# The end of the first block: additions to x ahead of the row scale's copy, and the row scale's fetch ahead of raw weight loads

## The chip, the cores and the metric

The kernel runs on one core of a Trainium2 chip. The metric is the device time of one execution in microseconds (us). Three runs of the kernel before took 599.77, 598.26 and 590.91 us; the median is 598.26. The core's engines are TensorE (PE: matmuls into PSUM banks), VectorE (DVE), ScalarE (ACT), GpSimd (POOL) and SyncE (SP). The last three also issue DMA transfers, each in the order of its own program.

## The reference

Two layers share one layernorm of x (2048 rows of 1024) and their results are added to x. The first is a diagonal complex state space model, the second a dense layer with the Mish activation.

```python
xn = layernorm(x)
# A: Lam_bar = exp(dt * Lam);  B_bar = ((Lam_bar - 1) / Lam)[:, None] * B
Bu = einsum("bld,pd->blp", xn, B_bar)
h[t] = Lam_bar * h[t - 1] + Bu[t]
a = 2 * einsum("blp,dp->bld", h, C).real + xn * Dskip
# B: w1 is 1024 x 3584, w2 is 3584 x 1024
m = mish(xn @ w1 + b1)
return x + a + m @ w2
```

## The kernel before, in words

**Blocks.** The 2048 rows are worked in four blocks of 512 (L1801 and on). Block 0 uses plain matmuls. In block 1 the product with B, and a part of the product with w1, are done in 2 x 2 halves with seven products instead of eight; the products are named by a letter and a number (`a2` is form 2 of the pair a). In blocks 2 and 3 all of w1 is done so. The seven products need sums and differences of halves of the weights, in f16, so the weights are first scaled by powers of two.

**Units of w1.** w1 is cut into seven units of 512 columns, numbered 0 to 6. A unit goes through a chain: `w_load` (L1089, four raw loads at L1096 on GpSimd's queue), `w_scale` (L1160, two scalings at L1163 on ScalarE, then three stores of raw parts to `wsd` in DRAM at L1157 on GpSimd), and `w_sums` (L1170, four sums at L1178 on VectorE, each followed by a store at L1157). The first sum writes over the raw part whose store is the third of `w_scale`. SyncE then loads the forms from `wsd` into the seven slots of `ring` (L457), in the order in which TensorE uses them. Unit 3 is loaded first at the end of block 0, then unit 4; units 5 and 6 follow in block 1, their loads standing on GpSimd's queue behind the stores of unit 3's sums.

**The row scale.** B's rows are scaled by powers of two before the seven products of block 1. `rows_scale` (L1726) works the scales out on VectorE and writes them to DRAM as `scd` (L1745); `rows_fetch` (L1748, the DMA at L1749) fetches them, spread over all partitions; `rows_spread` (L1753, the copy at L1754) puts them in order on VectorE; `scale_B` (L1766, products at L1771) multiplies B by them. Each is done for two halves. For half 0 the write and the fetch stand on GpSimd's queue, for half 1 on ScalarE's.

**The end of block 0.** `tail` (L1461) adds up the block's eight PSUM banks; its last matmuls (L1468) read the scanned state. `finish` (L1654) then adds two banks to a quarter of x on VectorE (L1665) and stores the result from ScalarE's queue (L1651). TensorE's next work is `first_tile` (L866): twelve tiles of w1 for block 1, of eight matmuls each (L873), tile f in bank f modulo 8; ScalarE empties each with Mish (L881). After them come the products of B in the order of `WHOLE` (L190: a2 a1 b2 b1 a5 b5 ...) at L950 and those of the units at L1022. The pair a uses banks 4 to 6 and the pair b banks 0 to 2: b2 writes bank 1, b1 bank 0, b5 bank 2.

**What sets the order.** Each engine's instructions are recorded in the order in which the Python program calls them, and run in that order; an instruction waits for the events of the buffers it reads and writes (`Queue`, L91 and on). `side(f)` (L1805) interleaves other work with the tiles: with tile 0 the sums of units 3 and 4 and the loads of units 5 and 6, and with tile 7 `w_scale(5)`, which on ScalarE thus stands ahead of emptying tiles 8 to 11.

Of the kernel before, what the change touches and what calls it, by code (L numbers as in the profile page):

```python
# [163 lines left out]
def build_kernel(nc, A_x, A_Lambda_re, A_Lambda_im, A_B_re, A_B_im, A_C_re, A_C_im,  # L164
# [16 lines left out]
    FAST = 1  # L181
# [95 lines left out]
    def c(n):  # L277
        return cs[:, CN.index(n), :]
# [963 lines left out]
    def some(n):  # L1242
        for _ in range(n):
            (steps or later).pop(0)()
# [481 lines left out]
    def rows_scale(h):  # L1726
        hs = slice(NJ // 2 * h, NJ // 2 * (h + 1))
        ab0, ab1, ss, si = (c(n)[:, hs] for n in ("ab0", "ab1", "ss", "si"))
        e8, f8 = si_i[:, 0, hs], si_i[:, 1, hs]
        b_a, b_e, b_f = b_ab[0][h], b_si_i[0][h], b_si_i[1][h]  # L1730

        def power(o, b_o, src, b_s, m, a):
            vop(lambda e: e.tensor_scalar(f8, src, m, a, op0=ALU.mult, op1=ALU.add), reads=[b_s], writes=[b_f])
            vop(lambda e: e.tensor_scalar(o.bitcast(i32), f8, 23, None, op0=ALU.logical_shift_left), reads=[b_f], writes=[b_o])

        vop(lambda e: e.tensor_tensor(ab0, ab0, ab1, op=ALU.add), reads=[b_a, b_ab[1][h]], writes=[b_a])
        vop(lambda e: e.tensor_scalar(ab0, ab0, 2.0 ** 100, 2.0 ** -100, op0=ALU.min, op1=ALU.max),
            reads=[b_a], writes=[b_a])
        vop(lambda e: e.tensor_scalar(e8, ab0.bitcast(i32), 24, None, op0=ALU.logical_shift_right),
            reads=[b_a], writes=[b_e])  # L1740
        power(ss, b_ss[h], e8, b_e, -2.0, 2.0 * 127 + 9)
        vop(lambda e: e.tensor_copy(sbf[:, hs], ss), reads=[b_ss[h]], writes=[b_sbf[h]])
        power(si, b_si[h], e8, b_e, 1.0, 59.0)
        power(ab1, b_ab[1][h], e8, b_e, -1.0, 195.0)
        (AC if h else PO).dma(lambda e: e.dma_start(scd[h], sbf[:, hs]), DmaSem(nc, "d_scd%d" % h),  # L1745
                              reads=[b_sbf[h]], writes=[b_scd[h]])
# [56 lines left out]
    for blk in range(NB):  # L1803

        def side(f):  # L1805
            if blk:
                if f == 0:
                    snaps_ready()
                    scale_B(1, (1,))
                    w_sums(3)  # L1810
                    w_load(5)
                    sums_B(0)
                    for n in range(4):
                        sums_x(blk, n)
                    sums_B(1)
                    w_load(6)
                    rows_spread(1)
                    scale_B(2)
                    w_sums(4)
                    scale_B(3)  # L1820
                if f in (1, 3, 4, 5):
                    table_scale((1, 3, 4, 5).index(f))
                if f == 7:
                    w_scale(5)
                    w_sums(5, True)
                ring_fill()
                return
            if f == 2:
                turn_sines()
            if f == NR:  # L1830
                aop(lambda e: e.activation(act[:, 0:NR, 0:2 * P], hraw[:, 0:NR, :], AF.Mish),
                    reads=b_hbf[0:4], writes=b_actf[0:NR])
            if f in (19, 27):
                for j in range(4):
                    table(j + (4 if f > 19 else 0))
            if f in (5, 6, 7, 8):
                coefficients(f - 5)
            if f in (8, 9, 11, 12):
                ln_skip(0, (8, 9, 11, 12).index(f))
            if f in turns:  # L1840
                transpose_B(turns.index(f))
            if f >= 26:
                transpose_C(f - 26)
            if f == 9:
                for h in range(2):
                    w_most(2, h)
            if f >= 12 and f % 4 < 2:
                w_most(f // 4, f % 4)
            if f in (23, 25, 26, 27):
                ln_stats_only(1, (23, 25, 26, 27).index(f))  # L1850
            if f == 26:
                w_row(0)
                w_spread(0)

        for x, f in enumerate(() if blk in SPLIT else TILES if blk == FAST else range(NF)):
            first_tile(blk, f)
            side(x)

        near = 0 < blk < NB - 1
        out_stage = tail(blk, n_item[0] + (len(W_ITEMS) if blk in SPLIT else len(OPENS) // 2 if blk == FAST else 0))  # L1860
        open_unit = next(out_stage)
        if blk in SPLIT:
            project_fast(blk, STEPS if near else LAST, open_unit)
        elif blk:
            project_fast(blk, WHOLE, open_unit)
        else:
            project_in()
        if blk == FAST:
            for q in range(NQ):
                next_stats(blk + 1, q)  # L1870
        if blk in SPLIT:
            next(out_stage)
            if near:
                next(out_stage)
        for j in range(NJ):
            if blk == 0 and j == NJ - 1:
                rows_scale(0)
                w_load(3)
                rows_fetch(0)
            if blk == 0 and j == 0:  # L1880
                w_exponent(0)
            recur(blk, j)
            if blk == FAST and j == 0:
                next_root()
                for q in range(NQ):
                    next_scale(blk + 1, q)
            if blk in SPLIT:
                if near and j == 0:
                    act_sums(blk, ((4, 0),))
                    next(out_stage)  # L1890
                if near and j in (2, 4, 7):
                    some(4)
                if j == 6:
                    vop(lambda e: e.tensor_tensor(KS[:, 1, :, :], KS[:, 1, :, :], KS[:, 3, :, :], op=ALU.add),
                        reads=[b_KS[1], b_KS[3]], writes=[b_KS[1]])
                continue
            if blk:
                if j == 0:
                    next(out_stage)
                    w_load(2)  # L1900
                    for i in range(2):
                        w_abs(i)
                    w_row(1)
                    w_spread(1)
                    w_scale(2)
                if j == 5:
                    w_exponent(1)
                    row_bound()
                    for i in range(2):
                        w_scale(i)  # L1910
                continue
            if j == 0:
                ln_root()
                for q in range(NQ):
                    ln_scale(1, q)
            scale_C(j)
            if j:
                keep_C(j - 1)
            if j < 3:
                next(out_stage)  # L1920
            if j < 4:
                for g in ((7,), (8,), (9, 10), (11,))[j]:
                    row_sizes(g)
            if j == 3:
                next(out_stage)
                for i in range(NHS):
                    rows_load(i)
                rows_size(0)
                rows_size(1)
                row_sizes(12)  # L1930
                rows_size(2)
                row_sizes(13)
                next(out_stage)
            for i in {4: (3, 4), 5: (5, 6, 7), 6: (8, 9, 10, 11), 7: range(12, 16)}.get(j, ()):
                rows_size(i)
        if near:
            for q in range(NQ):
                ln_skip(blk + 1, q)
            for n in range(4):
                sums_x(blk + 1, n)  # L1940
        if 0 < blk < NB - 1:
            carry()
        if blk == SPLIT[0]:
            uncarry()
        if blk == FAST:
            w_sums(2, True)
            some(4)
            for i in (0, 1):
                w_sums(i, True)
        if blk == FAST - 1:  # L1950
            keep_C(NJ - 1)
            w_load(4)
            rows_scale(1)
            for n in ("c1", "s1"):
                PO.op(lambda e, n=n: e.tensor_tensor(c(n), c(n), c("ab1"), op=ALU.mult), reads=[b_cs[n]] + b_ab[1], writes=[b_cs[n]])
            carry(PO)
            rows_spread(0)
            scale_B(0)
            scale_B(1, (0,))
            w_scale(3)  # L1960
            rows_fetch(1)
            w_scale(4)
        for _ in out_stage:
            pass

    SP.wait(out_events.values())

# [33 lines left out]
```

## Time and profile before

| what | value |
| --- | --- |
| median of three runs | 598.26 us |
| profiled execution, its own time | 598.32 us |
| its span | 597.1 us |
| TensorE busy | 583.7 us, 98% of the span |
| VectorE busy | 503.1 us, 84% |
| ScalarE busy | 403.5 us, 68% |
| GpSimd busy | 153.7 us, 26% |
| mean granted clock of TensorE | 0.997 |

The span runs from the first to the last instruction; the execution's own time is 1.2 us longer. A row of a timeline gives the start in us, the length in us, the engine, the line of the kernel, the operation, what is written and what is read, how many instructions are merged in the row, and in brackets how long the engine had stood idle and what ended that. In the chain of waits a row has the start, the length and what the chain ran through. In a list of waits a row has who waited for whom, the total in us, how often, and the longest. The granted clock is the share of TensorE's full rate that the chip allowed it.

### The profile page before, as it was taken

The page shows a single profiled execution, that of the slowest core. Times are in us where ns is not written, and L with a number is a line of the kernel's source. Part 1 is how long each engine was busy: PE and PEld are TensorE (multiplying, and loading weights), DVE is VectorE, ACT ScalarE, POOL GpSimd, SP SyncE. Part 2 cuts the span into 40 slices and gives each one's busy share as a digit, 9 for nine tenths or more (in the row PEclk, how much of TensorE's full clock was granted, in tenths as well). Part 3 has the DMA queues.
Part 4 walks back from the last instruction along what each step waited for, and adds up shares of the span by engine and source line. Part 5 has one row for each costly group of instructions (what it writes and reads, how often), then busy time and mean ns, then how long its engine had stood idle before and what let it go on. Part 6 is the DMA issues. An engine that isn't in the chain of part 4 may idle for free.

```text
span 597.1 us, 9755 instructions
## 1 busy us (share of the span) xinstructions
PE 583.7 (98%) x3606; PEld 354.1 (59%) x3643; DVE 503.1 (84%) x749; ACT 403.5 (68%) x540; POOL 153.7 (26%) x221
## 2 busy tenths in 40 slices
PE   8999999999969999999999999999999999999998
PEld 7644444444425888544448888744446888854444
DVE  6998787968798778999675869899999568789995
ACT  4879981979687877896505687889621798892330
POOL 2899300211554411340310321011510013100000
PEclk9999999999989999999999999999999999999999
DMA  9999999998799989889989968969985956989832
GB/s 251 250 259 232 195 196 223 265 384 291 173 302 296 342 287 316 276 314 292 194 317 384 305 216 265 297 235 286 314 329 188 395 185 221 335 299 344 298 117 71
DMA packets 115785, 160.32 MB, mean 269 GB/s; under 512 B 56074, under 2 KB 67082, under 8 KB 115738
## 3 DMA queue, kind: packets, MB, share of 16 engines
q1 hardware_dynamic: 97696, 105.99, 61.4%
q0 software_dynamic: 13520, 44.19, 22.4%
q10 hardware_dynamic: 4522, 9.52, 4.4%
q8 instruction: 29, 0.48, 0.3%
q14 instruction: 18, 0.15, 0.1%
HBM read 113.52 MB, written 34.08 MB: 247 GB/s over the span
## 4 chain that ended last, share of the span: by engine, by line
PE 70%; DVE 10%; SPq 9%; DMA 5%; ACT 3%; issue 3%; POOL 1%; POOLq 0%; DVEq 0%; ACTq 0%
PE ps L1468 27%; PE ps L1022 18%; PE ps L950 12%; PE ps L1527 8%; SPq L848 5%; PE ps L873 4%; SPq L842 3%; DMA ring<-in_B_w_dram 2%; DVE cs L1111 2%; DMA xx<-in_A_x_dram 1%; DVE CT L837 1%; DVE CT L835 1%; ACT hsink L1251 1%; DMA act<-scd 1%; DVE hT L1419 1%
## 5 line engine op out<-in xcount | busy, mean ns | idle before, releaser
L1468 PE MATMUL ps<-ring,act 128*128 128x512 bf16 x594 | 131.2, 379 | 2.0 <-DMA ring<-in_B_w_dram 1.3
L1468 PEld LDWEIGHTS ps<-ring,act 128*128 128x128 bf16 x608 | 59.4, 98 | 72.9 <-DMA ring<-in_B_w_dram 1.8
L1042 ACT ACTIVATE snaps<-ps,par,cs 128x256 f32<-128x256 f32 x98 | 53.3, 562 | 57.0 <-PE ps L1022 34.8
L1468 PE MATMUL ps<-ring,hT 128*128 128x512 bf16 x354 | 78.2, 379 | 0.4
L1022 PE MATMUL ps<-TT,ring 128*128 128x256 f16 x576 | 71.2, 273 | 0.0
L912 DVE TENSOR_TENSOR mt<-hT,tab 128x2048 bf16<-128x2048 bf16 (+1 forms) x56 | 67.9, 1213 | 0.4
L873 PE MATMUL ps<-xnT,ring 128*128 128x512 bf16 x258 | 58.1, 385 | 6.0 <-DVE xx L1665 5.8
L1468 PEld LDWEIGHTS ps<-ring,hT 128*128 128x128 bf16 x362 | 35.4, 98 | 42.7
L1419 DVE TENSOR_TENSOR_SCAN hT<-cs,qi,hT 128x512 bf16<-128x512 f32 x48 | 60.7, 1274 | 0.0
L1022 PEld LDWEIGHTS ps<-TT,ring 128*128 128x128 f16 (+1 forms) x576 | 56.2, 98 | 7.5 <-issue 0.2
L1059 DVE SCALAR_TENSOR_TENSOR act<-ps,cs,snaps 128x512 bf16<-128x512 f32 x54 | 39.9, 749 | 20.0 <-PE ps L1022 17.7
L1022 PE MATMUL ps<-xnT,ring 128*128 128x256 bf16 x432 | 54.5, 273 | 0.0
L873 PEld LDWEIGHTS ps<-xnT,ring 128*128 128x128 bf16 x264 | 26.1, 99 | 37.8 <-issue 8.0
L1022 PEld LDWEIGHTS ps<-xnT,ring 128*128 128x128 bf16 (+1 forms) x432 | 42.3, 98 | 5.3
L1206 POOL DMA_DIRECT2D w2d<-hb x28 | 20.0, 716 | 96.3 <-ACT hb L1216 53.3
L1439 ACT ACTIVATE hT<-hT,wz 128x1024 bf16<-128x1024 bf16 x16 | 17.9, 1144 | 27.5 <-DVE hT L1434 27.5
L896 ACT ACTIVATE act<-act 128x2048 bf16<-128x2048 bf16 (+3 forms) x12 | 32.8, 2756 | 4.8 <-DVE act L1045 4.7
L975 DVE TENSOR_TENSOR hT<-ps,snaps 128x512 f16<-128x512 f32 x36 | 23.9, 687 | 13.1 <-ACT snaps L967 11.5
L1251 ACT ACTIVATE hsink<-ring 128x1024 bf16<-128x1024 bf16 x28 | 29.5, 1054 | 6.0 <-DMA ring<-in_B_w_dram 4.9
L1157 POOL DMA_DIRECT2D wsd<-hb x35 | 19.0, 544 | 53.4 <-DVE hb L1178 32.1
L1163 ACT ACTIVATE hb<-hb,cs 128x2048 bf16<-128x2048 bf16 x10 | 19.4, 1994 | 16.2 <-DVE cs L1152 9.9
L1527 PE MATMUL ps<-ring,act 128*128 128x512 bf16 (+1 forms) x129 | 29.1, 379 | 0.2
(234 smaller groups left out, 1047.8 us busy)
## 6 DMA issues: line engine op xcount, KB each, us to landing
ring<-wsd SPq DMA_DIRECT2D x126, 256.0 KB, 5.3
ring<-in_B_w_dram SPq DMA_DIRECT2D x58, 512.0 KB, 5.8
ring<-ctd SPq DMA_DIRECT2D x24, 512.0 KB, 5.4
ring<-w2d SPq DMA_DIRECT2D x24, 512.0 KB, 5.1
wsd<-hb POOLq DMA_DIRECT2D x35, 256.0 KB, 5.2
w2d<-hb POOLq DMA_DIRECT2D x28, 256.0 KB, 4.9
hb<-in_B_w_dram POOLq DMA_DIRECT2D x20, 256.0 KB, 6.3
ctd<-CT ACTq DMA_DIRECT2D x8, 512.0 KB, 6.0
```

What stands on the lines that cost most here:

```text
L848: SP.dma(lambda e: e.dma_start_transpose(CT[:, :, ci, db * P:(db + 1) * P], src[db * P:(db + 1) * P, :]), s_CT, writes=b_CT + b_early)
L873: PE.mm(lambda e, k=k, w=w: e.matmul(ps[:, bank, :], lhsT=w, rhs=xnT[:, k, :], start=k == 0, stop=k == NK - 1), reads=[b_ring[s]] + b_xnT, ...
L896: aop(lambda e: e.activation(t, t, AF.Mish), reads=b, writes=b)
L912: vop(lambda e: e.tensor_tensor(mt[:], u.unsqueeze(1).to_broadcast([P, 2, 2, TB]), tab[:, :, j, :].unsqueeze(2).to_broadcast([P, 2, 2, TB] ...
L950: PE.mm(lambda e, w=w, x=x, o=o, begin=begin, end=end: e.matmul(ps[:, bank, o:o + TH], lhsT=w, rhs=x, start=opens and begin, stop=end, ski ...
L1022: PE.mm(lambda e, w=w, x=x, o=o, begin=begin, end=end: e.matmul(ps[:, bank, o:o + TH], lhsT=w, rhs=x, start=opens and begin, stop=end, ski ...
L1042: aop(lambda e, o=o, p=p, j=j: e.activation(o, p, AF.Identity, scale=ig, bias=b1(f0 + j)), reads=[b_ps[b], b_par, b_ig], writes=b_dst)
L1059: vop(lambda e: e.scalar_tensor_tensor(out=dst, in0=bank(b), scalar=ig, in1=src, op0=ALU.mult, op1=ALU.add), reads=[b_ps[b], b_snap[k], b_ ...
L1251: aop(lambda e, src=src, r=r: e.activation(hsink[:], src, AF.Abs, accum_out=wp[:, r:r + 1]), reads=[b_ring[s]], writes=b_hbf[2 * GF:] + [b ...
L1419: vop(lambda e: e.tensor_tensor_scan(out=hT[:, ci, j, :], data0=cj("r", j).to_broadcast([P, TB]), data1=hT[:, ci, j, :], initial=init, op0 ...
L1468: PE.mm(lambda e: e.matmul(ps[:, u, :], lhsT=lhsT, rhs=rhs, start=st_, stop=last, skip_group_check=blk in SPLIT), reads=reads, writes=[b_p ...
L1527: PE.mm(lambda e: e.matmul(ps[:, bank, :], lhsT=lhsT, rhs=rhs, start=st_, stop=end, skip_group_check=True), reads=b_t + [b_ring[s]], write ...
```

## The change

The fetch of the row scale's half 0 is called ahead of the raw loads of unit 3, so on GpSimd's queue it stands right behind the write that it waits for, and the loads behind it. And the copy of the row scale and the first three products with B are called after the end of the block's `tail`, so on VectorE the four additions to x stand ahead of them. On TensorE, ScalarE and SyncE the order of the instructions stays as it was.

```diff
@@ the scans of block 0
             if blk == 0 and j == NJ - 1:
                 rows_scale(0)
+                rows_fetch(0)
                 w_load(3)
-                rows_fetch(0)
@@ the end of block 0
             carry(PO)
-            rows_spread(0)
-            scale_B(0)
-            scale_B(1, (0,))
             w_scale(3)
             rows_fetch(1)
             w_scale(4)
         for _ in out_stage:
             pass
+        if blk == FAST - 1:
+            rows_spread(0)
+            scale_B(0)
+            scale_B(1, (0,))
```

## The prediction

> **What bounds the kernel now.** I read the page first, then the chain of waits around the change, then TensorE's waits, then the timelines of all five engines from 144 to 206 us.
>
> The page and TensorE's waits from 163 to 330 us:
>
> ```profile
> span 597.1 us, 9755 instructions
> PE 583.7 (98%) x3606; PEld 354.1 (59%) x3643; DVE 503.1 (84%) x749; ACT 403.5 (68%) x540; POOL 153.7 (26%) x221
> ...
> PE ps L873 <- DVE xx L1665: 5.8, 2, 5.6
> ```
>
> TensorE is busy for 98% of the span, so a change pays only where it closes a hole in PE. In that stretch PE waits for one thing only: 5.8 us, for VectorE's additions to x (L1665). The chain of waits shows what holds that addition back:
>
> ```profile
> 157.39 5.79 DMA act<-scd
> 163.20 0.44 DVE act L1754
> 163.76 1.24 DVE BT L1771
> ...
> 166.16 1.22 DVE BT L1771
> 167.38 1.15 DVE xx L1665
> 168.66 1.01 PE ps L873 x2
> ```
>
> The fetch of the row scale starts at 157.39 on GpSimd's queue. VectorE stands in front of its copy (L1754) until 163.20, does three products with B (L1771), and only then the first addition, which frees PSUM banks 0 and 1 for the first tile of block 1 (L873). PE itself had finished at 163.1 (143.73 + 19.37 in the next fence).
>
> PE's timeline:
>
> ```profile
> 143.73 19.37 PE L1468 MATMUL ps<-CT,hT 128*128 128x512 bf16 x88
> 168.66 1.01 PE L873 MATMUL ps<-xnT,ring 128*128 128x512 bf16 x2 [5.56 <-DVE xx L1665]
> 169.89 21.11 PE L873 MATMUL ps<-xnT,ring 128*128 128x512 bf16 x92 [0.22 <-DVE xx L1665]
> 190.84 3.66 PE L950 MATMUL ps<-xnT,BT 128*128 128x256 bf16 x32
> 194.33 3.66 PE L950 MATMUL ps<-TT,SS 128*128 128x256 f16 x32
> ```
>
> Twelve tiles of 8 matmuls (L873) are followed by the products a2, a1, b2, b1 (L950). 32 matmuls take 194.33 - 190.84 = 3.49 us, so b2, the third, starts at 190.84 + 1.75 = **192.59**. From there PE runs without a wait. So the question is when b2 can start.
>
> **Part one, the additions first.** Their rows on VectorE:
>
> ```profile
> 163.20 0.43 DVE L1754 COPY act<-act 128x512 bf16<-128x512 bf16 x1 [2.84 <-DMA act<-scd]
> 163.76 3.62 DVE L1771 TENSOR_TENSOR BT<-BT,act 128x2048 bf16<-128x2048 bf16 x3
> 167.30 4.61 DVE L1665 TENSOR_TENSOR xx<-ps,xx 128x1024 bf16<-128x1024 f32 x4
> 171.82 1.21 DVE L1771 TENSOR_TENSOR BT<-BT,act 128x2048 bf16<-128x2048 bf16 x1
> 172.99 2.87 DVE L1178 TENSOR_TENSOR hb<-hb 128x1024 f16<-128x1024 bf16 x4
> ```
>
> No work is added. The first addition needs the first quarter of PE's last 16 matmuls, 12 x 0.22 us (19.37/88) before 163.1, so it starts near 160.5, and the four end near 165.2. PE goes straight on at 163.1: the holes of 5.56 and 0.22 go. Then come the copy and the four products, 0.43 + 3.62 + 1.21, so VectorE is ready for the sums of w1's unit 3 (L1178) at about 170.5 instead of 172.99.
>
> PE's clock in and after the hole (columns: window; length, PE busy and matmuls; granted clock; DMA share; GB/s):
>
> ```profile
> 168.60:170.00 1.40, 1.12 (x3) 0.50 0.73 75
> 170.00:171.00 1.00, 1.00 (x3) 0.50 1.33 130
> 171.00:172.00 1.00, 1.00 (x4) 0.68 0.52 187
> 172.00:173.00 1.00, 1.00 (x7) 1.00 1.01 383
> ```
>
> After the hole PE has half its clock from 168.66 to 171 and 0.68 in the next microsecond: 0.5 x 2.34 + 0.32 = 1.5 us lost, of which I take 1.3, because PE's twelve tiles took 22.0 us for 96 matmuls that at the later rate of 0.216 would be 20.7. Without the hole the tiles end near 163.1 + 20.7 = 183.8 and b2 is due at **185.6**, 7.0 us (5.78 of wait, 1.3 of clock) earlier than before.
>
> **Part two, the fetch ahead of the raw loads.** GpSimd's rows; L1745 writes the scale, L1096 loads w1 raw, L1749 fetches the scale, L1157 stores units. The last two rows are an earlier write and fetch of the same kind:
>
> ```profile
> 152.89 0.54 POOL L1745 DMA_DIRECT2D scd<-sbf  x1 [7.91 <-DVE cs L1734]
> 153.43 2.99 POOL L1096 DMA_DIRECT2D hb<-in_B_w_dram  x4
> 157.39 0.55 POOL L1749 DMA_DIRECT2D act<-scd  x1 [0.96 <-DMA scd<-sbf]
> 157.93 2.97 POOL L1096 DMA_DIRECT2D hb<-in_B_w_dram  x4
> ...
> 167.05 0.54 POOL L1157 DMA_DIRECT2D wsd<-hb  x1 [0.77 <-ACT hb L1163]
> ...
> 173.97 0.54 POOL L1157 DMA_DIRECT2D wsd<-hb  x1 [1.42 <-DVE hb L1178]
> ...
> 176.68 2.98 POOL L1096 DMA_DIRECT2D act<-in_B_w_dram  x4
> ...
> 63.91 0.60 POOL L1134 DMA_DIRECT2D wmd<-cs  x1
> 67.97 0.54 POOL L1139 DMA_DIRECT2D wmx<-wmd  x1 [3.45 <-DMA wmd<-cs]
> ```
>
> GpSimd issues in order and the fetch waits for the write. Before, the four loads of unit 3 were issued inside that wait, for nothing. Now they stand behind it. The write takes 4.06 (63.91 to 67.97, alone on the queue) to 4.50 us (152.89 to 157.39), so the fetch starts at 156.95 to 157.39 and the loads at 157.5 to 157.95; I take 157.7, **4.3 us later**. The loads of unit 4 and the carry behind them move 3 us; the carry is read by the scans of block 1 after 250 us, so it costs nothing.
>
> ScalarE's rows show who waits for these loads (L1163 scales a raw unit, L881 empties a tile of block 1):
>
> ```profile
> 162.86 3.90 ACT L1163 ACTIVATE hb<-hb,cs 128x2048 bf16<-128x2048 bf16 x2 [5.22 <-DMA hb<-in_B_w_dram]
> 167.83 2.00 ACT L1163 ACTIVATE hb<-hb,cs 128x2048 bf16<-128x2048 bf16 x1 [1.07 <-DMA hb<-in_B_w_dram]
> 169.74 1.99 ACT L1163 ACTIVATE hb<-hb,cs 128x2048 bf16<-128x2048 bf16 x1
> ...
> 172.53 1.28 ACT L881 ACT_TABLE_LOAD   x1 [0.80 <-DVE xx L1665]
> ...
> 186.85 3.89 ACT L1163 ACTIVATE act<-act,cs 128x2048 bf16<-128x2048 bf16 x2 [2.03 <-DMA act<-in_B_w_dram]
> 190.65 2.40 ACT L881 ACTIVATE act<-ps,par 128x512 bf16<-128x512 f32 x4
> ```
>
> The last two rows matter most. ScalarE's order is fixed: tiles 0 to 7, then the scale of unit 5 (186.85, after a wait for its load), then tiles 8 to 11. Product b2 writes bank 1, which tile 9 holds; tile 9 is emptied at 190.65 + 2 x 0.60 = 191.85. Before, that was 0.74 us ahead of b2. Now PE comes 7 us earlier, and this is **what is late next**. Even with nothing moved, b2 could start only at 191.9, and the hole there would throttle the clock again.
>
> And unit 5 does move. The units share a chain, step by step:
> 1. Unit 3 lands. From first issue to its scale it was 153.43 to 162.86 = 9.43, for unit 4 157.93 to 167.83 = 9.90. So 157.5 + 9.43 = 166.9 to 157.95 + 9.90 = 167.85; I take 167.1, nearer the lower, as unit 3 goes first.
> 2. Scaled: + 3.90 = 171.0. The store of its last raw quarter follows, as before (166.76 to 167.05), at 171.3.
> 3. The first sum of L1178 writes over that quarter, so it waits until the store has landed. The store of 167.05, and those of 165.2 and 170.1, took, by issues in three small windows:
>
> ```profile
> DMA to landing us min/median/max: 5.8/5.8/5.8
> ...
> DMA to landing us min/median/max: 3.9/4.0/4.2
> ...
> DMA to landing us min/median/max: 5.7/6.0/6.3
> ```
>
>    With 5.8 the sums start at 171.3 + 5.8 = 177.1 (from 175.0 to 178.3 with the ends of steps 1 and 3) instead of 172.99, where the landing at 172.85 was just hidden. Behind them on VectorE wait the sums of B and of x, all 4.1 us later; a5 and b5, which read them, come 3.5 us behind b2, and these sums end before it.
> 4. Their four stores and then the load of unit 5 follow on GpSimd: 176.68 - 172.99 = 3.69, so 180.8.
> 5. Unit 5 lands after 186.85 - 176.68 = 10.17: 190.95 (with 9.43, the quickest unit: 190.2).
> 6. Its scale and two tiles, 3.80 + 1.20: tile 9 is empty at 195.95, and **b2 starts there, 3.35 us later than 192.59**.
> 7. PE has then stood for 10.3 us. The same clock loss follows as after the old hole, 1.3 us, now behind b2, where everything is on the path.
>
> The clock is worth a second look. The Trainium skill, "TensorE: Matmul & The Clock Gate", Part 1 (The HAM clock gate), says that an idle window of about 3.4 us halves the clock, and that about 3.4 us of work restore it. By it the loss would be 1.7 instead of my 1.3, and the sum 0.4 us higher; the trace shows the half rate for somewhat less time. It speaks against this change: the gap only moves, so the saving in clock is not one.
>
> **Sum.** 3.35 + 1.3 = +4.65 us on the profiled execution's 598.32 (span 597.1 and 1.2 around it), which is the median of the three runs, 598.26, within 0.1: **603.0 us**. The bounds: at the lowest of each step b2 comes at 175.0 + 3.69 + 9.43 + 5.0 = 193.1, +0.5, and no clock loss: 598.8. At the highest 178.3 + 3.69 + 10.17 + 5.0 = 197.2, +4.6 and 1.5: 604.4; add 1.5 for the four stores of the output, which now run at 171 to 175 beside the store of step 3: 605.9.
>
> Behind b2 nothing else should break. Unit 4's fifth form is the tightest: SyncE's queue waits for its store, loads it into the ring at 190.65, and PE wants it a product after 204.81.
>
> ```profile
> 190.65 3.60 SPq L457 DMA_DIRECT2D ring<-wsd  x5
> ...
> 204.81 1.91 PE L1022 MATMUL ps<-TT,ring 128*128 128x256 f16 x16
> DMA to landing us min/median/max: 3.8/6.4/7.9
> ```
>
> With the longest landing, 7.9, it was there at 198.6, 7.1 us before 205.7 (the landings are of those five loads). It moves with L1178 by about 4.1, and PE's need by 4.65.
>
> **The rivals.**
> A (the forecast): the gap moves to b2 and unit 5 is late. 603.0.
> B: the raw loads are not late where it counts, because their landing is set by something common. Then tile 9 is empty at 191.85, b2 starts at 191.9, 0.7 earlier, and the clock costs 1.3: +0.6, **598.9**. Against it: unit 4's loads, issued where unit 3's now go, landed in time for 167.83 and not sooner. The Trainium skill, "DMA: Bandwidth & Descriptors", Anatomy of one DMA (SWDGE path), gives 2.0 us and the bytes at 436 GB/s, an estimate of 2.6 us for 256 KB, by which unit 3 would land at 162.5 and this case would hold; the trace's rows disagree with 9.4 to 9.9 us from first issue to use.
> C, not slower: PE keeps what it gains, if unit 5 is early enough that ScalarE empties tiles 8 to 11 as PE fills them. 598.3 - 7.0 = **591.3**. For it is only that TensorE bounds the kernel. Against it: unit 5 would have to be scaled 7 us earlier, while its load is behind everything that moved later.
> D, much slower: unit 4's forms reach the ring too late, and p5/q5 stop PE. It decides from 7.1 us of extra delay on, at one us of time per us; to pass 2% it needs some 14 us of delay: **about 612**. Against it: 4.1 us, and PE's need moves too.
> That the change does nothing is out: the additions do stand ahead of the copy, and they wait for PE alone.
>
> **How the numbers follow.** A 0.70, B 0.10, C 0.13, D 0.07. The runs of before spread from 590.91 to 599.77, and 2%, 12 us, is about what a measurement can tell from no change. The range takes A's bounds and B, and some 2.8 us below and 0.6 above for that spread: 596.0 to 606.5; C and D, 2 in 10, are left out. Faster by over 2% (under 586.3) needs C and a favourable spread: 0.03. Slower by over 2% (over 610.2) is D: 0.07. The rest is within: 0.90.
>
> **What would show it.** Right: L873 starts near 163.1 at full clock; the additions run from 160.5; L1096 starts near 157.7; L1163 of unit 3 starts near 167; VectorE idles from 170.5 to 177 ahead of L1178; PE has a hole of some 10 us ahead of b2 (L950) put down to ScalarE's L881, and half clock after it. Wrong: L1163 near 163 (B), no hole ahead of b2 (C), or PE waiting for ring<-wsd in L1022 (D). The weakest terms are the landing of the store in step 3 and of unit 5.

## The result and the profile after

The changed kernel took a median of 604.1 us (22 runs, 594.84 to 615.89), the kernel before 598.24 us (22 runs, 589.79 to 609.41). Some executions of every kernel are some per cent longer, mostly at a lower granted clock, and the ratios here leave those out on both sides. The ratio is **1.0104, 95% interval 1.0064 to 1.0144**: 3.8 to 8.6 us slower, 6.2 in the middle. That is within 2%, and it is slower. The fastest runs of the two kernels lie 5.05 us apart. The forecast was 603.0 us, +4.65.

The page of the changed kernel:

```profile
span 600.0 us, 9754 instructions
PE 584.9 (97%) x3606; PEld 354.9 (59%) x3643; DVE 504.5 (84%) x749; ACT 402.9 (67%) x540; POOL 154.2 (26%) x221
```

TensorE's busy time grew by 1.2 us and its idle time by 1.7. Its timeline shows where:

```profile
161.95 20.88 PE L873 MATMUL ps<-xnT,ring 128*128 128x512 bf16 x94
182.67 1.91 PE L950 MATMUL ps<-xnT,BT 128*128 128x256 bf16 x16
192.63 3.57 PE L950 MATMUL ps<-xnT,BT 128*128 128x256 bf16 x16 [8.04 <-ACT act L881]
195.99 4.90 PE L950 MATMUL ps<-TT,SS 128*128 128x256 f16 x32
...
204.22 1.91 PE L1022 MATMUL ps<-xnT,ring 128*128 128x256 bf16 x16
```

The hole ahead of the first tile (L873) is gone. A larger one, 8.04 us, stands between a1 and b2, put down to ScalarE emptying a tile (L881). Behind it matmuls take almost twice as long: the row at 192.63 needs 3.36 us to the next start where the row at 204.22 needs 1.75.

TensorE's windows of the changed kernel (length, PE busy and matmuls, granted clock, DMA share, GB/s) give the clock there:

```profile
192.60:193.00 0.40, 0.37 (x2) 0.50 0.74 169
...
197.00:198.00 1.00, 1.00 (x7) 0.50 1.06 399
198.00:199.00 1.00, 1.00 (x9) 0.74 1.00 377
```

The clock is at half until past 198, more than 5 us. And the chain of waits of the changed kernel names the steps from unit 3's scale to b2:

```profile
167.20 2.00 ACT hb L1163
...
169.48 4.34 DMA wsd<-hb
...
173.92 0.70 DVE hb L1178
...
177.63 2.24 POOL act L1096 x3
179.86 7.55 DMA act<-in_B_w_dram
...
189.34 1.99 ACT act L1163
191.33 1.16 ACT act L881 x2
...
192.63 11.76 PE ps L950 x80
```

From below: b2 waits for the second of tiles 8 to 11 (L881), these for the scale of unit 5 (L1163), that for unit 5's load (L1096), that for the stores behind unit 3's sums (L1178), and the sums for the store of the raw part that the first sum writes over.

The list of waits has two rows for this one hole; VectorE's rows below them show how to choose:

```profile
PEld ps L950 <- DVE BT L1771: 8.3, 1, 8.3
PE ps L950 <- ACT act L881: 8.0, 1, 8.0
...
164.65 4.88 DVE L1771 TENSOR_TENSOR BT<-BT,act 128x2048 bf16<-128x2048 bf16 x4
184.19 0.69 DVE L1784 TENSOR_TENSOR BT<-BT 128x1024 f16<-128x1024 bf16 x1
190.53 2.48 DVE L1771 TENSOR_TENSOR BT<-BT,act 128x2048 bf16<-128x2048 bf16 x2
```

The weight load is put down to the products with B (L1771). Those of the pairs a and b had ended at 169.5 (164.65 + 4.88), and the last sum that writes to pair b's buffer (L1784) at 184.9, while TensorE stood from 184.6 to 192.6. The products of L1771 that run late in the hole, from 190.53, are for another pair, which b2 does not read. So it was not they that held b2: a name in this list is that of the event that came last by the profile, and need not be the cause.

**One clock for all runs.** Executions differ by 10 us and more in one place that the change does not touch: TensorE waits between 0 and 11.6 us for a load of w2 near 124 us. Behind it hangs the chain that ends in the row scale, so that the scale's write on GpSimd (L1745) comes anywhere from 146 to 163 us. I therefore read all times from the start of that write, "t0". The kernel before was profiled three times, the changed one twice:

| kernel | t0 | first tile | b2 - t0 | p1 - t0 | end of span - t0 |
| --- | --- | --- | --- | --- | --- |
| before | 152.89 | 168.66 | 39.7 | 48.4 | 444.2 |
| before, second | 152.23 | 167.87 | 39.6 | 48.4 | 444.4 |
| before, third | 154.47 | 169.91 | 39.2 | 48.0 | 444.3 |
| changed | 150.97 | 161.95 | 41.7 | 53.3 | 449.0 |
| changed, second | 159.52 | 171.62 | 42.4 | 53.8 | 450.0 |
| additions first alone | 154.47 | 164.51 | 38.0 | 48.7 | 444.8 |
| fetch first alone | 147.57 | 161.19 | 41.8 | 53.3 | 449.6 |
| changed, unit 5 late | 153.74 | 163.77 | 34.5 | 44.2 | 447.3 |
| additions first, unit 5 late | 156.03 | 167.60 | 34.0 | 42.8 | 440.4 |
| the same, second | 148.22 | 161.35 | 35.6 | 44.3 | 442.1 |
| before, unit 5 late | 145.98 | 162.29 | 38.8 | 47.5 | 444.1 |
| changed, PE kept busy | 162.75 | 175.34 | 42.8 | 51.6 | 447.4 |
| additions first, units 5 and 6 late | 147.01 | 161.47 | 36.9 | 45.7 | 448.2 |

b2 and p1 are the first matmuls of these products; where b2 stands inside a merged row, half of 3.5 us is added to the row's start. The change costs 4.7 to 5.8 us from t0 to the end (449.0 and 450.0 less 444.2 to 444.4); the forecast was +4.65, the timed middle 6.2. This clock is exact only while the chain behind the write sets the time. Where the write comes early, TensorE's own end of block 0 sets it: so two profiles of one kernel give 440.4 and 442.1, with the write 11.7 and 13.3 us ahead of that end.

### The profile page after: what moved, and what is told of

It reads as the page before. It is cut to its first block, busy times and chain, and to the rows that moved or that the text cites. A ratio compares the mean times of both kernels' runs of the same rounds, so it can differ in the third digit from the quotient of the medians.

```text
span 600.0 us, 9754 instructions
## 1 busy us (share of the span) xinstructions
PE 584.9 (97%) x3606; PEld 354.9 (59%) x3643; DVE 504.5 (84%) x749; ACT 402.9 (67%) x540; POOL 154.2 (26%) x221
## 4 chain that ended last, share of the span: by engine, by line
PE 66%; DMA 8%; DVE 8%; SPq 7%; POOL 5%; ACT 4%; issue 3%; ACTq 0%; POOLq 0%; DVEq 0%
PE ps L1468 27%; PE ps L1022 18%; PE ps L950 12%; PE ps L1527 8%; SPq L848 4%; DMA xx<-in_A_x_dram 2%; DMA ring<-in_B_w_dram 2%; SPq L842 1%; DMA scd<-sbf 1%; POOL py L764 1%; DMA act<-in_B_w_dram 1%; DVE CT L835 1%; POOL px L762 1%; DVE CT L837 1%; ACT hsink L1251 1%
## 5 line engine op out<-in xcount | busy, mean ns | idle before, releaser
L1042 ACT ACTIVATE snaps<-ps,par,cs 128x256 f32<-128x256 f32 x98 | 53.4, 563 | 55.1 <-PE ps L1022 32.8
L873 PE MATMUL ps<-xnT,ring 128*128 128x512 bf16 x258 | 56.8, 379 | 0.3
L873 PEld LDWEIGHTS ps<-xnT,ring 128*128 128x128 bf16 x264 | 25.8, 98 | 30.9
L975 DVE TENSOR_TENSOR hT<-ps,snaps 128x512 f16<-128x512 f32 x36 | 23.9, 687 | 15.0 <-ACT snaps L967 12.2
L1163 ACT ACTIVATE hb<-hb,cs 128x2048 bf16<-128x2048 bf16 x10 | 19.3, 1993 | 22.2 <-DVE cs L1152 12.7
L950 PE MATMUL ps<-xnT,BT 128*128 128x256 bf16 x192 | 24.9, 284 | 8.0 <-ACT act L881 8.0
L1251 ACT ACTIVATE hsink<-ring 128x1024 bf16<-128x1024 bf16 x28 | 29.5, 1054 | 3.5 <-DMA ring<-in_B_w_dram 2.3
```

The source lines that it names most:

```text
L873: PE.mm(lambda e, k=k, w=w: e.matmul(ps[:, bank, :], lhsT=w, rhs=xnT[:, k, :], start=k == 0, stop=k == NK - 1), reads=[b_ring[s]] + b_xnT, ...
L950: PE.mm(lambda e, w=w, x=x, o=o, begin=begin, end=end: e.matmul(ps[:, bank, o:o + TH], lhsT=w, rhs=x, start=opens and begin, stop=end, ski ...
L1042: aop(lambda e, o=o, p=p, j=j: e.activation(o, p, AF.Identity, scale=ig, bias=b1(f0 + j)), reads=[b_ps[b], b_par, b_ig], writes=b_dst)
L1251: aop(lambda e, src=src, r=r: e.activation(hsink[:], src, AF.Abs, accum_out=wp[:, r:r + 1]), reads=[b_ring[s]], writes=b_hbf[2 * GF:] + [b ...
```

## The experiments

**Each half alone.** The first of them keeps the fetch in its old place:

```diff
                 rows_scale(0)
-                rows_fetch(0)
                 w_load(3)
+                rows_fetch(0)
```

> The additions first, the fetch and the raw loads in the order of before. Read from the issue of the scale's write (L1745): before, b2 starts at 39.7 us and p1 (first L1022) at 48.4; changed kernel, 41.7 and 53.3. Theory (b2 waits for tile 9, which ScalarE empties behind the scale of unit 5): unit 5 is not later than before, so tile 9 is empty at about 39.0 as before and b2 starts at 39.1; PE has a hole of some 5 us ahead of b2 instead of ahead of the first tile, and the half clock behind it costs 1.3 to 2.9: p1 at 49.1 to 50.7, 0.7 to 2.2 us slower than before. Rival (the additions first pay, the raw loads alone cost): 7 us faster than before.

Median 598.52 us; ratio to before 0.9993, 0.9937 to 1.0048: no difference. TensorE's timeline of it:

```profile
164.51 20.88 PE L873 MATMUL ps<-xnT,ring 128*128 128x512 bf16 x96
...
192.45 3.57 PE L950 MATMUL ps<-xnT,BT 128*128 128x256 bf16 x16 [5.31 <-ACT act L881]
```

The hole is 5.31 us, where "some 5" was expected, and it stands ahead of b2. b2 starts 38.0 us after t0, 1.1 earlier than expected, and p1 at 48.7, expected at 49.1 to 50.7, against 48.0 to 48.4 before. So the additions first win nothing even by themselves: they move the hole over twelve tiles and two products to the next wait of the same length. The rival's 7 us are out.

The other half alone, in the kernel before:

```diff
                 rows_scale(0)
+                rows_fetch(0)
                 w_load(3)
-                rows_fetch(0)
```

> The fetch ahead of the raw loads, VectorE in the order of before. Theory: unit 3 is as late as in the changed kernel, so b2 starts at 41.7 us after the scale's write, while the first addition starts only about 1 us earlier than before; PE has two holes, some 4.5 us ahead of the first tile and some 3 ahead of b2; p1 at 50.4 to 53.3, 2 to 4.8 us slower than before. Rival (the fetch's place costs nothing, the order on VectorE does): no slower than before, b2 at or before 39.7.

Median 603.02 us; ratio 1.0083, 1.003 to 1.0137. b2 comes at 41.8 and p1 at 53.3, as in the changed kernel. **This half is the whole loss.** Two parts of the expectation missed: the hole ahead of b2 was 5.51 us, not some 3, and there was no hole ahead of the first tile, because in this execution the scale's write came at 147.57, 13.8 us ahead of TensorE's end of the block, and the additions, at 159.65, were in time. GpSimd's, ScalarE's and TensorE's rows of it:

```profile
151.39 0.54 POOL L1749 DMA_DIRECT2D act<-scd  x1 [3.28 <-DMA scd<-sbf]
151.92 5.95 POOL L1096 DMA_DIRECT2D hb<-in_B_w_dram  x8
...
161.87 2.00 ACT L1163 ACTIVATE hb<-hb,cs 128x2048 bf16<-128x2048 bf16 x1 [9.54 <-DMA hb<-in_B_w_dram]
...
187.95 2.40 ACT L881 ACTIVATE act<-ps,par 128x512 bf16<-128x512 f32 x4
...
189.33 3.57 PE L950 MATMUL ps<-xnT,BT 128*128 128x256 bf16 x16 [5.51 <-DVE BT L1771]
```

GpSimd stands for 3.28 us at the fetch, with eight loads behind it; unit 3 reaches ScalarE 14.3 us after t0, against 10.0 in the kernel before. The hole of 5.51 us ahead of b2 carries the name of L1771 again. Tile 9 is empty at 189.15 (187.95 and two of the four tiles), and b2 starts 0.18 us behind it, as in the changed kernel (192.44 to 192.63) and with the additions first alone.

**Is it ScalarE's order?** If b2 waits because tile 9 is emptied behind the scale of unit 5, that scale must go:

```diff
-                if f == 7:
-                    w_scale(5)
-                    w_sums(5, True)
...
-    WHOLE = ("a2 a1 b2 b1 a5 b5 P4 P5 a6 b6 v6 P6 ...
+    WHOLE = ("a2 a1 b2 b1 a5 b5 P4 P5 a6 b6 v5 v6 P6 ...
```

`v5` stands for both calls. First with the change as it is:

> The changed kernel with the scale of unit 5 behind the copies of a6 and b6 on ScalarE instead of ahead of emptying tiles 8 to 11. Theory: b2 no longer waits, PE runs from the first tile through p1 without a hole, p1 starts 40.5 us after the scale's write, 8 earlier than before; then p5/q5 may wait up to 2.4 us for unit 4's forms, which are 2.5 us later than before, and p6/q6 up to 2 for ScalarE. In all 4 to 8 us faster than before. Rival (b2 is held by the order on VectorE, by B's products, or by the transfers): the hole ahead of b2 stays and the time is that of the changed kernel.

Median 597.69 us; ratio 1.0031, 0.9979 to 1.0082. The 8.04 us ahead of b2 became 0.53, so the cause of the hole is shown. But the expected 4 to 8 us did not come. The waits of TensorE in it, from 160 to 250 us:

```profile
PE ps L1022 <- ACT snaps L1042: 2.1, 1, 2.1
PE ps L950 <- DVE hT L975: 1.4, 1, 1.4
PE ps L873 <- ACT act L881: 1.2, 1, 1.2
PE ps L950 <- ACT snaps L967: 0.8, 1, 0.8
PE ps L950 <- ACT act L881: 0.5, 1, 0.5
```

Every place where a late unit 3 or 4 shows takes a share: the first tiles are emptied late (L881), then the copies on ScalarE and VectorE. They add up to 6.0 us, and p1 came at 44.2 instead of 40.5. From t0 to the end this profile is 3 us longer than before (447.3). That all of these waits come from the late loads is read from the next run, in which they are nearly gone.

Then with the fetch in its old place as well, so that no load is late:

> The additions first, the fetch and raw loads in the order of before, and the scale of unit 5 behind the copies of a6 and b6 on ScalarE. Theory: no hole at the first tile or at b2, p1 40.5 us after the scale's write, and unit 4's forms not later than before, so p5/q5 wait for less than 1 us: 6 to 8 us faster than before, and 0 to 3 faster than the same with the fetch first. Rival as there: b2 still waits.

> The additions first, the fetch in its old place, unit 5's scale late, once more, for a second profile and more times. Theory: from PE's end of block 0 to the end of the span 428.5 to 429.5 us whatever happened before, against 434.0, 434.0 and 434.3 in the three profiles of before with a hole of over 5 us; the median of the times under that of before, but by less than 5 us, since not every execution of before has the hole. Rival: the 428.8 of the first profile was chance, and it takes 432 or more.

TensorE's waits of the first of these two, in the same stretch:

```profile
PE ps L1022 <- ACT snaps L1042: 0.4, 2, 0.2
PE ps L950 <- DVE hT L975: 0.3, 1, 0.3
```

The rival is out: 0.7 us of waits are left, b2 follows a1 without a hole, and from TensorE's end of block 0 (the first tile, where no hole is) to the end of the span it takes 428.8 and, in the second profile, 590.3 - 161.35 = 428.95 us, against 434.0 in the kernel before (597.1 - 163.1). Against the changed kernel with unit 5 late, the fetch's place alone is worth 5.2 to 6.9 us in these profiles from t0 to the end (447.3 less 442.1 and 440.4), where 0 to 3 were expected. The medians are 595.18 and 592.25 us, beside 596.38 and 596.94 for the kernel before in the same sessions: 1.2 and 4.7 less. But the ratios are 1.0012 (0.9964 to 1.006) and 0.9967 (0.9923 to 1.0011). So the 6 to 8 us expected from the first are **not in the times**, and neither interval excludes no change.

**Why the times don't show it.** The second and the third profile of before:

> The kernel before once more, for a second profile of it. One execution had the hole of 5.8 us ahead of the first tile, where PE ended 10.3 us after the scale's write. Theory: the first addition comes 14.4 us after the scale's write, so the hole is 15.8 us less the time from that write to PE's end of the block, and it differs from execution to execution with the start of that write. Rival: the hole is 5.8 us in every execution.

> The same as the run ahead of it, for a third profile: by the theory the hole again follows from the time between the scale's write and PE's end of the block (15.8 less that time); by the rival it is 5.8 us.

TensorE's hole in the second profile, after the end of the block at 134.99 + 27.79:

```profile
134.99 27.79 PE L1468 MATMUL ps<-CT,hT 128*128 128x512 bf16 x126
167.87 1.01 PE L873 MATMUL ps<-xnT,ring 128*128 128x512 bf16 x2 [5.09 <-DVE xx L1665]
```

In the two the write came 10.6 and 10.2 us ahead of TensorE's end. The rule gives holes of 5.2 and 5.6; measured were 5.09 and 5.24. These do not tell the two theories apart, since the interval hardly differed from the first profile's 10.2. The next kernel does, since up to the first tile it is the kernel before:

> The kernel before with only the scale of unit 5 moved behind the copies of a6 and b6. Theory: with the copy and the products ahead of the additions, tile 9 was already empty before b2 was due, so nothing is won: the hole ahead of the first tile stays, b2 starts 23.9 us after the first tile as before, and ScalarE's later order costs 0 to 1 us. Rival (the place of unit 5's scale alone holds the kernel): 4 us or more faster than before.

Its edit is the diff above on the kernel before. Median 593.02 us; ratio 1.0015, 0.9951 to 1.0078: the place of unit 5's scale alone changes nothing in the times, as expected. Its row on TensorE:

```profile
162.29 20.88 PE L873 MATMUL ps<-xnT,ring 128*128 128x512 bf16 x94 [0.90 <-DVE xx L1665]
```

Here the write came at 145.98, 15.4 us ahead of TensorE's end at 161.4, and the hole is 0.9 us, where the rule gives 0.4 and the expectation had it stay. b2 came 22.5 us after the first tile instead of 23.9. So the hole of 5.8 us, which the change was to close, is **not in every execution**: it is the lateness of the row scale against TensorE, and that lateness comes from the load of w2. Two rows from far above in the chain of waits of the kernel before show the link, the load and the sums of row sizes on ScalarE that wait for it:

```profile
112.73 12.16 DMA ring<-in_B_w_dram
124.92 1.16 ACT hsink L1251 x2
```

ScalarE waits 4.38 us there for that load, TensorE 1.30. The load delays the scale by more than it delays TensorE, and that opens the hole. All thirteen profiles fit: ScalarE waits 0 to 0.7 us for loads of w2 (L1251) where the write comes at 146.0 to 148.2, and 2.3 to 15.3 us where it comes at 151.0 to 162.8.

Where the load is early, this kernel runs its last 429 us as well as the best variant does (590.1 - 161.4 = 428.7). That the kernel before does so too is an inference: by its own rows tile 9 would be empty 39.0 us after the write, at 184.9 (191.85 - 152.89 after 145.98), 0.2 us behind the start of b2 here. The fastest timed runs of one session agree with it, 590.5 us for the kernel before and 590.58 for the best variant. That this is why the medians meet is not shown, since the timed runs have no profiles.

**The clock.** The changed kernel with TensorE kept busy in the hole, by matmuls into a bank that is free:

```diff
-    WHOLE = ("a2 a1 b2 b1 ...
+    WHOLE = ("a2 a1 K36 b2 b1 ...
+            elif kind == "K":
+                for i in range(n):
+                    PE.mm(lambda e, i=i: e.matmul(ps[:, 7, :], lhsT=BT[:, 0, 0, i % NK, :], rhs=xnT[:, i % NK, :],
+                                                  start=True, stop=True),
+                          reads=[b_BT[0]] + b_xnT, writes=[b_ps[7]], first=i == 0, last=i == n - 1)
```

> The changed kernel with 36 more matmuls into the free bank 7 between a1 and b2, work that nothing uses, so that PE is not idle in the hole. Theory (the hole costs its lateness and then a half clock): b2 starts as in the changed kernel, 41.7 us after the scale's write, but p1 8.7 us behind b2 instead of 11.6: 2.9 us faster than the changed kernel. Rival (the slow stretch behind b2 is PE waiting for weights or data): b2 to p1 stays at 11.6 us.

Median 598.36 us; ratio to before 1.0093, 1.0054 to 1.0131, which the times do not tell from the changed kernel's 1.0104. The profile does:

```profile
205.57 1.91 PE L950 MATMUL ps<-xnT,BT 128*128 128x256 bf16 x16
...
214.31 1.91 PE L1022 MATMUL ps<-xnT,ring 128*128 128x256 bf16 x16
```

From b2 to p1 it is 8.74 us, against 204.22 - 192.63 = 11.59 in the changed kernel, at a granted clock of 1.00 throughout. So 2.85 us of the loss are the half clock and nothing else; data and weights were in time. The filler ended when b2 started, at 205.6, about 1.5 us after tile 9 was empty (198.88 + 5.2 by the changed kernel's rows), so b2 was late by the filler itself, and the gain to the end of the span is 1.7 to 2.6 us rather than 2.9.

**Two more.** Unit 6 later too, on top of the best variant:

```diff
-    a6 b6 v5 v6 P6 ... p6 q6 P2 T4 p3 P3 q3 p7 q7 k0 c2 d2 p4 q4 T5 k0 k0 k0 m0
+    a6 b6 v5 P6 ... p6 q6 P2 T4 v6 p3 P3 q3 p7 q7 c2 d2 p4 q4 T5 k0 k0 k0 k0 m0
```

> The additions first, the fetch in its old place, the scale of unit 5 behind the copies of a6 and b6 and now the scale of unit 6 later too, behind the table scale that stands after q6, with the first sum of unit 6 two products later. In the run with unit 5 alone moved, PE still lost 1.2 us in small waits for ScalarE's and VectorE's copies between p1 and q6. Theory (ScalarE, 3.9 us behind, causes them): they go, and from PE's end of block 0 to the end of the span it takes 427.5 to 428.5 us instead of 428.8. Rival: the later unit 6 makes w1/w5 wait for the ring, 2 to 5 us more.

Median 596.89 us; ratio 1.0061, 1.0005 to 1.0118; 595.2 - 161.47 = 433.7 us from the first tile to the end. Neither side had it right: it lost 4.9 us against 428.8, as much as the rival said, but not at the ring. TensorE's waits from 161 to 330 us have 0.4 us for it, and that for a load of w2; the rest is ScalarE's copies (L1042) and VectorE's sums (L975). That unit 6's scale, 3.9 us long at its new place on ScalarE, holds these up is likely but not shown. Three of the rows:

```profile
PE ps L1022 <- ACT snaps L1042: 2.3, 2, 1.4
PE ps L1022 <- DVE hT L975: 1.7, 1, 1.7
...
PE ps L1468 <- DMA ring<-in_B_w_dram: 0.4, 1, 0.4
```

And the changed kernel a second time:

> The changed kernel once more, for a second profile. Theory: b2 starts 41 to 42.5 us after the scale's write wherever that write falls, and then half a clock for 3 to 6 us; from PE's end of block 0 to the end of the span 437 to 440 us, 3 to 6 more than before with its hole. Rival: the hole ahead of b2 was chance, under 434.

```profile
131.57 12.59 PE L1468 MATMUL ps<-ring,act 128*128 128x512 bf16 x47 [7.77 <-DMA ring<-in_B_w_dram]
...
201.94 3.57 PE L950 MATMUL ps<-xnT,BT 128*128 128x256 bf16 x16 [7.68 <-ACT act L881]
```

TensorE waited 7.77 us for the load of w2, everything is some 9 us later, and the hole ahead of b2 is there again, 7.68 us, with b2 42.4 us after t0 and 609.5 - 171.62 = 437.9 us to the end. The hole is not chance.

No variant here is shown to beat the kernel before. The best candidate is the additions first with unit 5's scale late and the fetch where it was.

## Why the prediction was right

The time, the sign and the mechanism were right; that the sum came so close is in part luck. Step by step, with the changed kernel's rows on GpSimd, ScalarE and VectorE:

```profile
150.97 0.55 POOL L1745 DMA_DIRECT2D scd<-sbf  x1 [7.91 <-DVE cs L1734]
154.41 0.54 POOL L1749 DMA_DIRECT2D act<-scd  x1 [2.90 <-DMA scd<-sbf]
154.94 5.96 POOL L1096 DMA_DIRECT2D hb<-in_B_w_dram  x8
...
177.62 2.99 POOL L1096 DMA_DIRECT2D act<-in_B_w_dram  x4
...
165.29 2.00 ACT L1163 ACTIVATE hb<-hb,cs 128x2048 bf16<-128x2048 bf16 x1 [9.57 <-DMA hb<-in_B_w_dram]
187.44 3.89 ACT L1163 ACTIVATE act<-act,cs 128x2048 bf16<-128x2048 bf16 x2 [4.21 <-DMA act<-in_B_w_dram]
...
159.56 4.62 DVE L1665 TENSOR_TENSOR xx<-ps,xx 128x1024 bf16<-128x1024 f32 x4 [0.68 <-PE ps L1468]
173.92 2.87 DVE L1178 TENSOR_TENSOR hb<-hb 128x1024 f16<-128x1024 bf16 x4 [4.39 <-DMA wsd<-hb]
```

- **The additions first.** They start 2.5 us before TensorE's end of the block, as forecast, and TensorE goes on without a hole.
- **The fetch, and step 1.** The fetch starts 3.44 us after the write (forecast 4.06 to 4.50), so the loads start 3.97 after t0 instead of 0.54: 3.4 later rather than 4.3. But unit 3 took 10.35 us from first issue to its scale (165.29 - 154.94), above the forecast's 9.43 to 9.90. The two misses cancel: unit 3 is scaled 14.32 after t0 instead of 9.97, 4.35 later, against 4.2.
- **Step 3, the term that was too large.** Step 2 held: from its scale to its third store unit 3 took 4.19 us (forecast 4.2). The store landed after 4.4 us (169.48 to 173.92) instead of 5.8, inside the range of 3.9 to 6.3. The sums start 22.95 after t0 instead of 20.10, 2.85 later instead of 4.1.
- **Steps 4 to 6.** 3.70 us (forecast 3.69), 9.82 (10.17) and 5.19 (5.0). b2 comes 1.96 us later after t0 than before; the forecast was 3.35. TensorE's hole ahead of it was 8.04 us, not 10.3.
- **Step 7, the term that was too small.** The half clock cost 2.85 us, not 1.3. I had taken its length from the earlier hole, where it lasted under 3 us; here it lasted over 5. The Trainium skill's 3.4 us ("TensorE: Matmul & The Clock Gate", Part 1), which gave an estimate of 1.7, was nearer than my row and still too low against the 2.85 measured.
- **The sum.** 1.96 + 2.85 = 4.8 at p1 (53.25 less 48.43) against 4.65: right in all by luck, since a term 1.4 too large and one 1.55 too small met. Behind p1 nothing was added: from p1 to the end it took 395.8 us before and after.
- **Rival B** fell with the scale of unit 3 at 14.3 us after t0, **C** with the hole ahead of b2, **D** since TensorE never waited for the ring there.
- **What the prediction lacked.** It read the hole ahead of the first tile from one execution, as if it were in all. The third profile's and the unit-5 kernel's rows show that the hole is 5 us or 1, by the load of w2. The loss does not hang on that hole, because the late unit chain starts at the scale's write itself. From t0 to the end it took 444.1 us where the hole was 0.9 us (the kernel before with unit 5 late) and 444.2 to 444.4 where it was over 5; with the fetch first it took 449.0 to 450.0, and 449.6 in the one execution with no hole to close. The forecast lies inside the timed 3.8 to 8.6; that their middle, 6.2, is higher, no run here explains.

## What to carry to other kernels

A wait on the busy engine is worth closing only as far as the next wait behind it: before moving work ahead, look for the next instruction that reads a buffer owned by another engine, and ask when that is free. An instruction that waits on an in-order queue is cheap only with work issued ahead of it; moving the waiter forward makes everything behind it pay the wait, here 3.4 us of a DRAM write and, through loads, scales, stores and sums, 4.7 to 5.8 at the end. And take a hole from several executions before counting on it, from a common event on.

## What the runs showed of the hardware that I had not expected

- The half clock after a hole is not of one length. After holes of 5.56 and 8.04 us it lasted under 3 and over 5 us; with the fetch first alone, after 5.51 us, until 195, again over 5:

```profile
189.00:190.00 1.00, 0.67 (x4) 0.50 0.97 254
...
195.00:196.00 1.00, 1.00 (x11) 0.92 0.97 307
```

  So its cost, 1.3 to 2.9 us here, does not follow from the hole's length, and an idle stretch moved to another place may cost more there. The Trainium skill ("TensorE: Matmul & The Clock Gate", Part 1) calls the activity window free-running and the count of slow matmuls variable from run to run; the lengths here agree with the second, no run here shows the window itself, and over 5 us is more than the 3.4 or so that it gives for the busy stretch.
- 36 matmuls that compute nothing needed took all of that cost away (8.74 us from b2 to p1 instead of 11.59), at a granted clock of 1.00.
